# Attention and two MoE layers: the remainder `gl` of the activations subtracted on DVE in place of POOL

## The chip, the cores and the metric

The kernel runs on one core of a Trainium2 chip. The metric is the device time of one execution in microseconds (us), lower is better. Engines are named as in the profile: PE (TensorE matmul), PEld (its weight loads), DVE (VectorE), ACT (ScalarE), POOL (GpSimd), SP (SyncE, which issues most DMAs).

## The reference

Three layers follow each other: attention with a soft cap on its scores, a first MoE layer, and a second one with a softmax and a layer norm. The change lies in the first MoE layer, `_moe_ref`.

```python
def _moe_ref(x, w_in, w_out):          # x 1792x768, w_in 768x2048, w_out 2048x768
    h = x @ w_in
    g = h - np.tanh(h)
    return (g @ w_out).astype(np.float32)
...
    attn_out = _attn_ref(**attn_kwargs)                  # batch 4, 12 heads, 448 x 64
    x = attn_out.transpose(0, 2, 1, 3).reshape(B * S, H * D)
    x = _moe_ref(x=x, **moe_kwargs)
    return _moe2_ref(x=x, **moe2_kwargs)
```

All results are float32. The kernel gets float32-like precision from three matmuls in a shorter format (float32r): every operand `x` is split into a rounded part `xh` and the remainder `xl = x - xh`, and `x·w` is computed as `xh·wh + xl·wh + xh·wl`.

## The kernel before, in words

The 1792 tokens are worked in two halves of 896 (`hb` 0 and 1). Each half passes through `attention`, `moe1` and `moe2`, with x held transposed in SBUF (six pairs of tiles `xh`, `xl`, 128 x 896).

`moe1` cuts the 2048 hidden columns into four chunks `c` of 512. `up(c, half)` makes two hidden tiles each, so there are four tiles `hp` per chunk, each 128 hidden columns x 896 tokens, with 36 matmuls of 448 columns (lines 403 and 405). Chunk 0 is made by `first()` while the attention's last heads still finish. An `hp` lies in PSUM. Chunks 1 to 3 use the pool with the tag "a", which has two buffers, so the third tile of a chunk needs the buffer of the first, and PE waits until ACT and DVE have read that first tile for the last time.

`nonlinear(c, hp)` turns each `hp` into g. There are 4 chunks x 4 tiles x 2 halves = 32 calls. ACT makes `u` (line 431, square), `t` (433, tanh), the mask `mk` (435) and `w` (439). DVE makes `gf` in three steps: line 437 and line 440 read `hp` out of PSUM (440 is the last reader and sets the buffer free), line 441 reads `w` and `gf`, and line 442 copies `t` over `gf` where the mask says so. Then ACT rounds `gf` to `gh` (line 445), and the remainder `gl = gf - gh` is made at line 446. `gh` and `gl` have six buffers each, `gf`, `u`, `t` and `mk` two, `w` one.

`down(c)` multiplies the four pairs `gh`, `gl` of a chunk with `w_out` (lines 459 and 461, 24 matmuls for each of six row tiles `d`), and adds the result to `acc` (line 466 for chunk 0, line 468 on DVE for the others). The program order is `first`, then for each chunk `up(c+1)` before `down(c)`.

The weights come as float64 words. In the first half each unit of 128 x 512 is converted on the way: SP loads the words `st` (three buffers), DVE narrows them to `f` (lines 106, 107, 108), ACT rounds (line 114), DVE subtracts the rest (line 115), and SP stores the pair to DRAM (line 131, `keep`). There are 13 + 1 buffers `w` and `wx` for pairs. In the second half the stored pairs are only loaded (line 186). So DVE carries the conversions beside `nonlinear` in the first half and not in the second.

In `attention` the order of the instructions is written out by hand. In `moe1` and `moe2` a scheduler orders the instructions of each engine from the program order and its own estimates of durations; each engine then runs its own list strictly in order.

Of the kernel before, what the change touches and what calls it, by code (L numbers as in the profile page):

```python
# [9 lines left out]
F32 = mybir.dt.float32  # L10
# [4 lines left out]
ALU = mybir.AluOpType  # L15
# [14 lines left out]
def fused_kernel(ctx, tc, qk_in, v, cap, w1, w2, w3, w4, gln, out):  # L30
    nc = tc.nc
# [35 lines left out]
    def pst(name, tag="b"):  # L67
        return psum[tag].tile([P, 2, 512], F32, tag=tag, name=name)
# [128 lines left out]
    def load_w1(c, half):  # L197
        ts = []
        for i in range(NK // 2):
            ts += cols(unit(f"1_{c}_{half}_{i}", w1u[(c * 2 + half) * (NK // 2) + i], 2), 2)  # L200
        return ts

    def load_w2(c, d):
        return cols(unit(f"2_{c}_{d}", w2u[c * NK + d], CH // P), CH // P)
# [186 lines left out]
    def moe1(mp, xh, xl, yh, yl):  # L391
        acc = [mp.tile([P, HT], F32, tag=f"acc{d}", name=f"acc{d}", bufs=1) for d in range(NK)]
        gs = {}
        place.update(pool=(mp, WX1), at=-1)

        def up_mms(hp, wt, m, k0, k1, gg=(0, 1)):
            ms = slice(m * P, (m + 1) * P)
            for kk in range(k0, k1):
                wh, wl = wt[kk]
                xs = [(xh[kk][:, g * S:(g + 1) * S], xl[kk][:, g * S:(g + 1) * S]) for g in range(2)]  # L400
                for i in range(2):
                    for g in gg:
                        nc.tensor.matmul(hp[:, g, :S], wh[:, ms], xs[g][i], start=(kk == 0 and i == 0), stop=False)  # L403
                for g in gg:
                    nc.tensor.matmul(hp[:, g, :S], wl[:, ms], xs[g][0], start=False, stop=(kk == NK - 1))  # L405

        def first():

            gs[0] = []
            wts = [load_w1(0, 0), load_w1(0, 1)]  # L410
            hps = [pst("hp", "ab"[half]) for half in range(2) for _ in range(2)]
            for g, k0, k1 in ((0, 0, NK), (1, 0, 3), (1, 3, 4), (1, 4, 5), (1, 5, 6)):
                for m in range(3):
                    up_mms(hps[m], wts[m // 2], m % 2, k0, k1, (g,))
                    if k1 == NK and g == 1:
                        nonlinear(0, hps[m])
            up_mms(hps[3], wts[1], 1, 0, NK)
            nonlinear(0, hps[3])

        def up(c, half):  # L420
            gs.setdefault(c, [])
            wt = load_w1(c, half)
            for m in range(2):
                hp = pst("hp", "a")
                up_mms(hp, wt, m, 0, NK)
                nonlinear(c, hp)

        def nonlinear(c, hp):
            h = hp[:, :, :S]
            u = mp.tile([P, 2, S], F32, tag="u", name="u")  # L430
            nc.scalar.activation(u, h, AF.Square)
            t = mp.tile([P, 2, S], F32, tag="t", name="t")
            nc.scalar.activation(t, h, AF.Tanh)  # L433
            mk = mp.tile([P, 2, S], U8, tag="mk", name="mk")
            nc.scalar.activation(mk, t, AF.Square, scale=TS)
            gf = mp.tile([P, 2, S], F32, tag="gf", name="gf")
            nc.vector.scalar_tensor_tensor(gf, u, C2, h, ALU.mult, ALU.mult)  # L437
            w = mp.tile([P, 2, S], F32, tag="w", name="w", bufs=1)
            nc.scalar.activation(w, u, AF.Square, bias=gat)
            nc.vector.tensor_tensor(t, h, t, ALU.subtract)  # L440
            nc.vector.scalar_tensor_tensor(gf, w, GB, gf, ALU.add, ALU.mult)
            nc.vector.copy_predicated(gf, mk, t)
            gh = mp.tile([P, 2, S], F32R, tag="gh", name="gh", bufs=6)
            gl = mp.tile([P, 2, S], F32R, tag="gl", name="gl", bufs=6)
            nc.scalar.copy(gh, gf)  # L445
            nc.gpsimd.tensor_tensor(gl, gf, gh.bitcast(F32), ALU.subtract)  # L446
            gs[c].append((gh, gl))

        def down(c):
            for d in range(NK):  # L450
                wt = load_w2(c, d)
                op = pst("op")
                nm = CH // P
                for m in range(nm):
                    gg = gs[c][m]
                    wh, wl = wt[m]
                    for i in range(2):
                        for g in range(2):
                            nc.tensor.matmul(op[:, g, :S], wh, gg[i][:, g], start=(m == 0 and i == 0), stop=False)  # L459
                    for g in range(2):  # L460
                        nc.tensor.matmul(op[:, g, :S], wl, gg[0][:, g], start=False, stop=(m == nm - 1))  # L461
                for g in range(2):
                    cs = slice(g * S, (g + 1) * S)
                    a = acc[d][:, cs]
                    if c == 0:
                        nc.scalar.copy(a, op[:, g, :S])
                    else:
                        nc.vector.tensor_tensor(a, op[:, g, :S], a, ALU.add)  # L468
                    if c == NCHUNK - 1:
                        nc.scalar.copy(yh[d][:, cs], a)  # L470
                        nc.vector.tensor_tensor(yl[d][:, cs], a, yh[d][:, cs].bitcast(F32), ALU.subtract)

        first()
        for c in range(NCHUNK):
            if c + 1 < NCHUNK:
                up(c + 1, 0)
                up(c + 1, 1)
            down(c)
# [192 lines left out]
```

## Time and profile before

| what | value |
|---|---|
| time, median of 3 runs | 979.12 us (975.68 to 985.18) |
| profiled execution, its own time | 978.58 us |
| its span, first to last instruction | 976.6 us |
| granted TensorE clock, mean over the span | 0.99 of full speed |
| busy in the span: PE / DVE / ACT / POOL | 938.9 / 607.8 / 420.5 / 125.9 us |
| POOL's 32 subtractions at line 446 | 76.4 us, mean 2395 ns |

The span is that of the profiled execution; 2.0 us of its time lie around it. Busy time of an engine is the time in which at least one of its instructions ran. A granted clock of 1.00 is 2.4 GHz, and 0.50 would be 1.2 GHz; a mean between the two means that part of the stretch ran at the lower level.

### The profile page before, as it was taken

Reading aid. Unit: us, or ns where it says so; the run is one execution under the profiler, and the core shown is the slowest. Engines: PE = TensorE matmul, PEld = TensorE weight load, DVE = VectorE, ACT = ScalarE, POOL = GpSimd, SP = SyncE. Lnnn points to the kernel's source line nnn. Section 1 sums busy time; section 2 is a strip of 40 time slices with the busy share of each in tenths; the row PEclk is TensorE's granted clock in tenths of the full one; section 3 lists DMA queues with packets and bytes.
Section 4 is the critical chain, followed back from the end, with each engine's and each line's share of the span. In section 5 each row is a group of like instructions: output and inputs, shape, how many; then the busy total and the mean of one; then the engine's idle time right before and its main releaser. Section 6 shows DMA issues by size and latency. Waiting matters only on the chain.

```text
span 976.6 us, 11710 instructions
## 1 busy us (share of the span) xinstructions
PE 938.9 (96%) x4512; PEld 756.1 (77%) x4512; DVE 607.8 (62%) x914; ACT 420.5 (43%) x502; POOL 125.9 (13%) x123
## 2 busy tenths in 40 slices
PE   6999969899899999999989999999999999999998
PEld 3444449798899998888865555789999999988887
DVE  4687676998999997389415675596044352405751
ACT  6878506644624323243238775085251331212321
POOL 2221001302212120001011210032110201000000
PEclk9999989999999999999999999999999999999999
DMA  6564275279676575244135652242323332303311
GB/s 240 179 174 153 88 273 207 70 234 312 240 249 251 210 282 195 98 159 154 49 112 182 190 168 77 93 134 104 108 87 130 108 109 87 108 21 109 125 50 48
DMA packets 48947, 145.66 MB, mean 149 GB/s; under 512 B 11708, under 2 KB 16188, under 8 KB 48892
## 3 DMA queue, kind: packets, MB, share of 16 engines
q1 hardware_dynamic: 41404, 114.57, 34.0%
q0 software_dynamic: 7344, 30.35, 9.7%
q8 instruction: 35, 0.57, 0.2%
q14 instruction: 20, 0.16, 0.1%
q10 hardware_dynamic: 144, 0.00, 0.0%
HBM read 98.73 MB, written 43.33 MB: 145 GB/s over the span
## 4 chain that ended last, share of the span: by engine, by line
PE 82%; DMA 9%; DVE 5%; ACT 2%; issue 1%; SPq 0%; DVEq 0%; ACTq 0%
PE op L459 14%; PE hp L403 13%; PE o L308 8%; PE op L461 7%; PE hp L405 7%; DMA rs<-ou 4%; PE hp L222 4%; PE hp L221 4%; PE hp L220 4%; PE s L274 4%; PE oab L556 2%; PE oab L560 2%; PE oab L557 2%; DMA rd<-rs 2%; PE s L276 1%
## 5 line engine op out<-in xcount | busy, mean ns | idle before, releaser
L403 PE MATMUL hp<-xh,w 128*128 128x448 f32 x384 | 118.5, 377 | 18.2 <-DVE t L440 8.3
L446 POOL TENSOR_TENSOR gl<-gf,gh 128x896 fp32r<-128x896 f32 x32 | 76.4, 2395 | 418.6 <-ACT gh L445 389.9
L308 PE MATMUL o<-t,vf 128*65 128x448 f32 x288 | 116.8, 543 | 2.8 <-issue 1.4
L403 PE MATMUL hp<-xl,w 128*128 128x448 f32 x384 | 119.0, 376 | 0.4 <-DVE xl L357 0.4
L405 PE MATMUL hp<-xh,w 128*128 128x448 f32 x384 | 117.5, 373 | 0.0
L278 ACT ACTIVATE t<-s,tscale 128x896 f32<-128x896 f32 x96 | 82.4, 913 | 41.6 <-PE s L274 27.0
L459 PE MATMUL op<-gh,w 128*128 128x448 f32 x336 | 95.5, 366 | 0.0
L461 PE MATMUL op<-gh,w 128*128 128x448 f32 x336 | 95.4, 365 | 0.0
L459 PE MATMUL op<-gl,w 128*128 128x448 f32 x336 | 95.4, 365 | 0.0
L403 PEld LDWEIGHTS hp<-xh,w 128*128 128x128 f32 x384 | 73.7, 193 | 27.2 <-issue 10.8
L437 DVE SCALAR_TENSOR_TENSOR gf<-u,hp 128x896 f32<-128x896 f32 x32 | 34.8, 1087 | 80.2 <-ACT t L433 80.2
L308 PEld LDWEIGHTS o<-t,vf 128*65 128x65 f32 x288 | 37.6, 137 | 58.8 <-issue 47.8
L403 PEld LDWEIGHTS hp<-xl,w 128*128 128x128 f32 x384 | 74.3, 193 | 9.8 <-issue 1.7
L405 PEld LDWEIGHTS hp<-xh,w 128*128 128x128 f32 x384 | 73.9, 193 | 7.9 <-issue 1.5
L288 ACT ACTIVATE t<-t,shift,capt 128x1792 f32<-128x1792 f32 (+1 forms) x48 | 78.5, 1687 | 0.0
L468 DVE TENSOR_TENSOR acc<-op,acc 128x448 f32<-128x448 f32 x72 | 42.0, 621 | 52.2 <-PE op L461 52.2
L114 ACT CAST w<-f 128x512 fp32r<-128x512 f32 x44 | 27.1, 620 | 104.5 <-DVE f L108 50.7
L459 PEld LDWEIGHTS op<-gh,w 128*128 128x128 f32 x336 | 63.0, 188 | 5.3 <-DVE acc L468 0.4
L459 PEld LDWEIGHTS op<-gl,w 128*128 128x128 f32 x336 | 63.1, 188 | 5.0
L461 PEld LDWEIGHTS op<-gh,w 128*128 128x128 f32 x336 | 63.1, 188 | 5.0
L220 PE MATMUL hp<-w,xh 128*128 128x512 f32 x168 | 65.5, 390 | 0.0
L221 PE MATMUL hp<-w,xh 128*128 128x512 f32 x168 | 65.4, 389 | 0.0
(135 smaller groups left out, 1730.0 us busy)
## 6 DMA issues: line engine op xcount, KB each, us to landing
d<-w SPq DMA_DIRECT2D x69, 512.0 KB, 4.3
w<-d SPq DMA_DIRECT2D x56, 512.0 KB, 3.3
st<-in_moe_w_out_dram SPq DMA_DIRECT2D x35, 512.0 KB, 5.7
st<-in_moe_w_in_dram SPq DMA_DIRECT2D x24, 512.0 KB, 4.5
kq<-in_qk_dram POOLq DMA_DIRECT2D x21, 480.0 KB, 4.3
w<-d POOLq DMA_DIRECT2D x13, 512.0 KB, 5.4
vf<-in_v_dram POOLq DMA_DIRECT2D x24, 260.0 KB, 5.2
st<-in_moe_w_in_dram POOLq DMA_DIRECT2D x12, 512.0 KB, 6.4
```

The source lines that it names most:

```text
L220: nc.tensor.matmul(ps, sh, mh, start=first, stop=False)
L221: nc.tensor.matmul(ps, sh, ml, start=False, stop=False)
L222: nc.tensor.matmul(ps, sl_, mh, start=False, stop=last)
L278: nc.scalar.activation(t[:, 2 * r:2 * r + m], s[:, :m, :S], AF.Tanh, scale=tscale)
L288: nc.scalar.activation(t[:, sl], t[:, sl], AF.Exp, bias=shift, scale=capt)
L308: nc.tensor.matmul(o, vf[:, r + 5 * hh], t[:, 2 * r + hh], start=(r == 0), stop=False)
L403: nc.tensor.matmul(hp[:, g, :S], wh[:, ms], xs[g][i], start=(kk == 0 and i == 0), stop=False)
L405: nc.tensor.matmul(hp[:, g, :S], wl[:, ms], xs[g][0], start=False, stop=(kk == NK - 1))
L446: nc.gpsimd.tensor_tensor(gl, gf, gh.bitcast(F32), ALU.subtract)
L459: nc.tensor.matmul(op[:, g, :S], wh, gg[i][:, g], start=(m == 0 and i == 0), stop=False)
L461: nc.tensor.matmul(op[:, g, :S], wl, gg[0][:, g], start=False, stop=(m == nm - 1))
L468: nc.vector.tensor_tensor(a, op[:, g, :S], a, ALU.add)
```

## The change

One line changes: the subtraction that makes `gl` is issued to DVE in place of POOL. Its operands and result stay.

```diff
             gh = mp.tile([P, 2, S], F32R, tag="gh", name="gh", bufs=6)
             gl = mp.tile([P, 2, S], F32R, tag="gl", name="gl", bufs=6)
             nc.scalar.copy(gh, gf)
-            nc.gpsimd.tensor_tensor(gl, gf, gh.bitcast(F32), ALU.subtract)
+            nc.vector.tensor_tensor(gl, gf, gh.bitcast(F32), ALU.subtract)
             gs[c].append((gh, gl))
```

The scheduler lays the other instructions out anew around it. On DVE, in the first half, from the second tile of chunk 0 on, the order before is this (`hp_1071`, `hp_1072`, `hp_1073` are the second to fourth tile of chunk 0; `f` and `w` with numbers from 1637 up are weight conversions):

```order
L440 TENSOR_TENSOR t_1198<-hp_1071,t_1198 128x896
L441 SCALAR_TENSOR_TENSOR gf_1202<-w_1204,gf_1202 128x896
L106 TENSOR_SCALAR f_1676<-st_1674 128x512
L442 COPY_PREDICATED gf_1202<-mk_1200,t_1198 128x896
L437 SCALAR_TENSOR_TENSOR gf_1222<-u_1216,hp_1072 128x896
L440 TENSOR_TENSOR t_1218<-hp_1072,t_1218 128x896
L107 SCALAR_TENSOR_TENSOR f_1676<-st_1674,f_1676 128x512
L441 SCALAR_TENSOR_TENSOR gf_1222<-w_1224,gf_1222 128x896
L437 SCALAR_TENSOR_TENSOR gf_1275<-u_1269,hp_1073 128x896
L442 COPY_PREDICATED gf_1222<-mk_1220,t_1218 128x896
L440 TENSOR_TENSOR t_1271<-hp_1073,t_1271 128x896
```

At the same place the order now is this:

```order
L440 TENSOR_TENSOR t_1198<-hp_1071,t_1198 128x896
L446 TENSOR_TENSOR gl_1190<-gf_1182,gh_1189 128x896
L441 SCALAR_TENSOR_TENSOR gf_1202<-w_1204,gf_1202 128x896
L437 SCALAR_TENSOR_TENSOR gf_1222<-u_1216,hp_1072 128x896
L442 COPY_PREDICATED gf_1202<-mk_1200,t_1198 128x896
L440 TENSOR_TENSOR t_1218<-hp_1072,t_1218 128x896
L446 TENSOR_TENSOR gl_1210<-gf_1202,gh_1209 128x896
L441 SCALAR_TENSOR_TENSOR gf_1222<-w_1224,gf_1222 128x896
L437 SCALAR_TENSOR_TENSOR gf_1275<-u_1269,hp_1073 128x896
L442 COPY_PREDICATED gf_1222<-mk_1220,t_1218 128x896
L440 TENSOR_TENSOR t_1271<-hp_1073,t_1271 128x896
```

Each tile's `gl` stands behind the next tile's line 440, in a group of five that repeats up to the second tile of chunk 1, and the conversion instructions that stood between (L106, L107, later L115 and L108) have moved behind these groups.

On PE, at the border between the second and the third tile of chunk 1 in the first half (`hp_1340` and `hp_1394`), the order before is this:

```order
L403 MATMUL hp_1340<-xh_105,w_730 128x448 x2
L403 MATMUL hp_1340<-xl_111,w_730 128x448 x2
L405 MATMUL hp_1340<-xh_105,w_730 128x448 x2
L403 MATMUL hp_1394<-xh_100,w_799 128x448 x2
L403 MATMUL hp_1394<-xl_106,w_799 128x448 x2
```

Now it is this:

```order
L403 MATMUL hp_1340<-xh_105,w_730 128x448 x2
L403 MATMUL hp_1340<-xl_111,w_730 128x448 x2
L405 MATMUL hp_1340<-xh_105,w_730 128x448 x2
L459 MATMUL op_1502<-gh_1189,w_960 128x448 x2
L459 MATMUL op_1502<-gl_1190,w_960 128x448 x2
L461 MATMUL op_1502<-gh_1189,w_960 128x448
L403 MATMUL hp_1394<-xh_100,w_799 128x448 x2
L403 MATMUL hp_1394<-xl_106,w_799 128x448 x2
```

Five of the six matmuls with which `down(0)` begins have moved ahead of the third tile; the same holds in the second half. The rest of PE's order is unchanged.

## Rows read from the trace of the kernel before

**Rows 1.** The page, part 1: engines' busy us, share of span, instructions.
```profile
PE 938.9 (96%) x4512; PEld 756.1 (77%) x4512; DVE 607.8 (62%) x914; ACT 420.5 (43%) x502; POOL 125.9 (13%) x123
```

**Rows 2.** Timeline of PE, rows with waits in moe1: start, duration, [idle before <-releaser].
```profile
181.81 0.64 PE L403 MATMUL hp<-xh,w 128*128 128x448 f32 x2 [3.32 <-DVE t L440]
191.47 0.64 PE L403 MATMUL hp<-xh,w 128*128 128x448 f32 x2 [0.50 <-DVE t L440]
247.24 0.64 PE L403 MATMUL hp<-xh,w 128*128 128x448 f32 x2 [4.46 <-DVE t L440]
...
659.67 0.65 PE L403 MATMUL hp<-xh,w 128*128 128x448 f32 x2 [1.92 <-issue]
```

**Rows 3.** Timeline of DVE around the wait in the second half.
```profile
658.47 1.09 DVE L440 TENSOR_TENSOR t<-hp,t 128x896 f32<-128x896 f32 x1
```

**Rows 4.** Stretches behind PE's waits: length, busy by engine, PEclk, DMA share, GB/s.
```profile
181.80:187.10 5.30, 5.29 (x19) 4.79 (x20) 5.30 (x6) 3.12 (x4) 1.60 (x2) 0.68 0.30 89
...
247.20:254.70 7.50, 7.46 (x29) 6.84 (x30) 7.50 (x11) 5.37 (x7) 3.92 (x1) 0.77 0.72 223
...
659.70:667.10 7.40, 7.40 (x29) 6.76 (x30) 5.38 (x5) 3.53 (x4) 3.17 (x2) 0.77 0.08 30
```

**Rows 5.** The two stretches up to the long wait; busy PE, PEld, DVE, ACT, POOL.
```profile
156.70:199.00 42.30, 38.48 (x179) 34.47 (x178) 42.13 (x40) 30.28 (x36) 14.87 (x6) 0.96 0.24 86
199.00:247.20 48.20, 43.78 (x217) 40.23 (x215) 42.56 (x64) 21.94 (x35) 4.88 (x2) 1.00 0.87 289
```

**Rows 6.** Timeline of POOL, first subtraction of the first half.
```profile
162.76 2.13 POOL L446 TENSOR_TENSOR gl<-gf,gh 128x896 fp32r<-128x896 f32 x1 [67.82 <-ACT gh L445]
```

**Rows 7.** Timeline of DVE beside it.
```profile
160.04 1.22 DVE L442 COPY_PREDICATED gf<-mk,t 128x896 f32<-128x896 uint8 x1
161.14 1.08 DVE L437 SCALAR_TENSOR_TENSOR gf<-u,hp 128x896 f32<-128x896 f32 x1
162.13 1.09 DVE L440 TENSOR_TENSOR t<-hp,t 128x896 f32<-128x896 f32 x1
163.14 2.69 DVE L441 SCALAR_TENSOR_TENSOR gf<-w,gf 128x896 f32<-128x896 f32 x1
```

**Rows 8.** DVE by lines, 156.5 to 250 us: xcount, busy us, mean ns, idle before.
```profile
L108 DVE SCALAR_TENSOR_TENSOR f<-st,f 128x512 uint32<-128x512 uint32 x17 | 14.6, 859 | 0.2
L441 DVE SCALAR_TENSOR_TENSOR gf<-w,gf 128x896 f32<-128x896 f32 x9 | 14.4, 1604 | 0.1
L115 DVE TENSOR_TENSOR w<-f,w 128x512 fp32r<-128x512 f32 x16 | 14.1, 881 | 2.1 <-ACT w L114 2.1
L107 DVE SCALAR_TENSOR_TENSOR f<-st,f 128x512 uint32<-128x512 uint32 x18 | 13.5, 755 | 0.3
```

**Rows 9.** Single lines over the whole span: ns min/median/max of one instruction.
```profile
L441 DVE SCALAR_TENSOR_TENSOR gf<-w,gf x32: 1074/1092/3022, 157.9 to 795.8; 128x896 f32<-128x896 f32 x32
L440 DVE TENSOR_TENSOR t<-hp,t x32: 1072/1082/1120, 158.9 to 796.9; 128x896 f32<-128x896 f32 x32
L107 DVE SCALAR_TENSOR_TENSOR f<-st,f x72: 677/693/2608, 11.0 to 440.2; 128x512 uint32<-128x512 uint32 x72
L115 DVE TENSOR_TENSOR w<-f,w x44: 671/684/2629, 142.1 to 376.8; 128x512 fp32r<-128x512 f32 x44
L445 ACT CAST gh<-gf x32: 938/944/953, 161.7 to 819.6; 128x896 fp32r<-128x896 f32 x32
```

**Rows 10.** Timeline of DVE ahead of the long wait.
```profile
243.07 0.42 DVE L106 TENSOR_SCALAR f<-st 128x512 uint32<-128x512 uint32 x1
243.41 1.08 DVE L437 SCALAR_TENSOR_TENSOR gf<-u,hp 128x896 f32<-128x896 f32 x1
244.41 0.68 DVE L107 SCALAR_TENSOR_TENSOR f<-st,f 128x512 uint32<-128x512 uint32 x1
245.01 1.08 DVE L441 SCALAR_TENSOR_TENSOR gf<-w,gf 128x896 f32<-128x896 f32 x1
246.01 1.08 DVE L440 TENSOR_TENSOR t<-hp,t 128x896 f32<-128x896 f32 x1
```

**Rows 11.** Weight words `st`, 140 to 260 us: issue to landing.
```profile
DMA to landing us min/median/max: 4.2/5.7/10.9
```

## The prediction

> **What bounds the kernel now.** I read the page's busy times first: PE is busy for 938.9 of 976.6 us, DVE for 62%, POOL for 13% [rows 1]. So PE sets the end, and a change on DVE or POOL counts only where PE waits for it. Next I went through PE's timeline for its waits in the first MoE layer. There are four [rows 2]: 3.32, 0.50 and 4.46 us in the first half, all released by line 440 on DVE, the last reader of an `hp` tile, and 1.92 us in the second half. The page labels the last one "issue", but line 440 ran until 658.47 + 1.09 = 659.56 [rows 3], just before PE went on at 659.67, so I count it with the others. Together they make 10.20 us. The third view is the granted clock behind these waits [rows 4]: after the three longer ones PE ran for a while at the lower of its two levels (1.2 in place of 2.4 GHz), with means of 0.68, 0.77 and 0.77. That costs 5.30 x 0.32 + 7.50 x 0.23 + 7.40 x 0.23 = 1.7 + 1.7 + 1.7 = 5.1 us more. After the wait of 0.50 us I count none. All that can be won here is thus 15.3 us.
>
> Why is DVE late? In the stretch up to the first two waits it is busy for 42.13 of 42.30 us [rows 5]. But its instructions are not all of their usual length. When POOL makes the first `gl` (162.76 to 164.89 [rows 6]), line 441, which starts at 163.14, takes 2.69 us [rows 7], against a median of 1.09 over the kernel [rows 9]. Line 440, one of whose inputs lies in PSUM, never takes more than 1.12 us [rows 9]. So POOL's subtraction holds up those DVE instructions that read two operands from SBUF.
>
> **What the change removes.** Up to 250 us there are eight `gl` on POOL. The slowed lines, mean against median [rows 8, 9]: L441 9 x (1.604 - 1.092) = 4.6; L115 16 x (0.881 - 0.684) = 3.2; L108, with L107's median as it has the same shape, 17 x (0.859 - 0.693) = 2.8; L107 18 x (0.755 - 0.693) = 1.1. That is 11.7 us, 1.5 us for each `gl`.
>
> **What it adds.** The trace has no DVE `gl`. The nearest row is L441, of the same shape with two inputs from SBUF: 1.07 us at its fastest, 1.09 in the median, 1.60 as the mean of the stretch with slowed ones [rows 8, 9]. Nothing on POOL is left in this layer to slow it, so I take the median. Consecutive instructions overlap a little: from L437 to L440 to L441 the starts lie 0.99 and 1.01 us apart [rows 7], so a `gl` occupies DVE for 1.0 us (bounds 1.0 to 1.5). Each also waits for `gh`. The cast on ACT takes 0.94 us [rows 9], and POOL took up the result at 162.76, about 0.1 us behind its end (161.7 + 0.94 [rows 6, 9]). In the new order, line 440 of the next tile stands between line 442 and the `gl`, which covers 1.0 of that. I count 0 to 0.1 us a `gl`, if ACT is free.
>
> By the Trainium skill (Perfetto Trace Analysis, Optimizing Scalar/DVE Operations), work may be moved off a saturated DVE, even to GPSIMD, and that advice speaks against this change. The same passage adds that the two share a port, and SBUF — State Buffer (Who interferes with whom) says that a DVE instruction with two SBUF inputs and a GpSimd one that reads SBUF exclude each other for a whole instruction. By that L441 at 163.14 would end about 1.09 us behind 164.89, so after 2.84 us; 2.69 were measured [rows 7], and the trace agrees with the second rule.
>
> **Place 1, third tile of chunk 1, first half (181.81).** The DVE order in the change section runs without conversions from line 440 at 162.13. Up to line 440 of chunk 1's first tile come 15 instructions, which start 0.99 to 1.10 us apart (1.10 behind L442 [rows 7]): 163.1 + 11 x 1.0 + 3 x 1.1 = 177.4 for the start, 178.5 for the end, 178.8 with three waits for `gh`. PE finishes the second tile at 181.81 - 3.32 = 178.5, and now has five matmuls of `down(0)` to do first, about 1.0 us (36 matmuls of one tile take some 7.4 us [rows 4]). It asks for the buffer at 179.5, 0.7 us after it is free. The wait goes, and with it the slow clock, and the 0.50 behind it. Gain 3.3 + 1.7 + 0.5 = 5.5 us. The five matmuls themselves are only moved.
>
> **Place 2, third tile of chunk 2 (247.24).** PE now arrives 5.5 us earlier, at 242.8 - 5.5 = 237.3. DVE has, up to line 440 (start 246.01 [rows 10]): 11.7 us of slowing less, 8 `gl` = 8.0 us more, and fewer conversion instructions ahead of it. Counted in the two orders, 34 L106, 34 L107, 33 L108, 19 L115 stood before it, and 31, 31, 31, 17 do now. With 0.34 for an L106 and 0.60 for the others (starts at 243.07, 243.41; 244.41, 245.01 [rows 10]) this is 3 x 0.34 + 7 x 0.60 = 5.2 us. Line 440 ends 8.9 us earlier, at 238.2, and PE waits 0.9 in place of 4.46 us. This supposes that the weight words come in time: the DMA engines are 0.87 busy here [rows 5], and a load takes 5.7 us in the median and 10.9 at most [rows 11]. I take a wait of 1.5 to 2 us and half of the slow clock: 4.46 + 1.7 - 1.8 - 0.8 = 3.6 us gained.
>
> **Later in the first half.** DVE stays nearly full up to the end of chunk 3, and PE comes 9 us earlier than before. The conversions that were put behind must be done here, but POOL's last six subtractions stop slowing DVE too. I take 0.5 us of new waits (0 to 3).
>
> **Place 3, second half (659.67).** The order is the same without conversions, so place 1's reckoning holds: 1.9 + 1.7 = 3.6 us gained.
>
> Sum: 5.5 + 3.6 - 0.5 + 3.6 = 12.2 us. 978.58 - 12.2 = 966.4, made against the profiled execution, which is 0.54 us under the median of the runs shown, so I round to 966.5. POOL's 76 us are worth nothing by themselves: nobody waits for POOL.
>
> **Rivals.**
>
> *The loads set the pace.* Three buffers of `st` make a conversion wait for a landing, and with landings towards 10.9 us [rows 11] in place of 5.7 the 11 loads between place 1 and place 2 (four rounds of three) take 4 x 2.3 = 9 us more than DVE needs, which eats the 8.9 us. Then PE reaches 247.24 as before, the first half gains nothing, and only 3.6 us of the second remain: 975. For it: the DMA share of 0.87 and DVE's 5.6 us of idle time in that stretch [rows 5]. Against: DVE then slept for little of it, and the worst landing is one of many.
>
> *DVE blocks itself (slower).* An in-order DVE that reaches a `gl` before its `gh` stands still, with line 440 of later tiles and the conversions queued behind, and PE waits for these. This happens where ACT has other work between line 442 and the cast, one or two instructions of about 0.9 us. The 12 `gl` up to chunk 3's first tile, each delayed by 2 us, cost 24 us, against about 8 us that DVE saves there (as at place 2: 8.9 us after eight `gl`): 16 us more in the first half, less 3.6 in the second: 991. It decides from about 0.7 us a `gl` on (8/12); the new order, with a line between 442 and the `gl`, speaks against.
>
> *The load alone counts.* If the long L441 had another cause than POOL, DVE would get 8 us of `gl` and no relief up to place 2, less the 5.2 us of conversions put behind: it would be 2.8 us later there, and 3 us (three `gl`) later at places 1 and 3. With 2 x 3 + 3 that makes 988. Rows 7 and 9 speak against it.
>
> *Nothing measurable.* The two long waits reappear elsewhere in the first half, as DVE is full there either way, and new small waits eat the second half's gain: 979.
>
> **How the numbers follow.** A measurement of this kernel tells about 1% from no change. 1% under the median is 969.3. Forecast (963 if every wait goes, 978.58 - 15.3, to 972): 0.56, of which 0.46 lies under 969.3. The loads: 0.18, within 1%. Nothing measurable: 0.12, within 1%. DVE blocks itself: 0.10, slower. The load alone: 0.04, of which 0.02 is slower by over 1% (988 lies at 0.9%). So faster 0.46; slower 0.12; within 1% 0.42. The range reaches from 962 to 978: it takes in the forecast and the loads' case and leaves out the last three, of which the nothing case lies at its edge. The forecast's own range is 963 to 972.
>
> **What would show it.** Right: L441, L107, L108 and L115 at 1.09, 0.69 and 0.68 us without outliers; L446 on DVE at about 1.09; no wait of PE for L440 near 179 and near 657; a short one near 238; clock 1.00 behind them. Wrong: L446 rows on DVE with idle time released by line 445; new PE waits between 250 and 320; a wait near 238 to 247 of several us with DVE idle for `st`.

## The result and the profile after

| | before | after |
|---|---|---|
| time, median | 978.83 us (973.42 to 985.18, 6 runs) | 965.97 us (961.69 to 968.56, 6 runs) |
| ratio, 95% interval | | 0.9894 (0.9862 to 0.9926) |
| profiled execution, its time / span | 978.58 / 976.6 us | 963.42 / 961.1 us |
| granted TensorE clock, mean of the span | 0.990 | 0.996 |

The changed kernel is faster by 1.1%. The forecast was 966.5 us in a range of 962 to 978.

The page's first part, which answers to [rows 1]: POOL's 75.8 us are gone, and DVE has only 4.2 us more, although it does 32 more instructions of 1.09 us (34.9 us). The missing 30.7 us are time that DVE's older instructions no longer take.

```profile
PE 935.8 (97%) x4512; PEld 751.5 (78%) x4512; DVE 612.0 (64%) x946; ACT 420.6 (44%) x502; POOL 50.1 (5%) x91
```

That is seen line by line in the single lines of DVE over the whole span (ns min/median/max of one instruction), which answer to [rows 9]. The medians are the same as before to about 1%, but the maxima of 2.6 to 3.0 us are gone. The new line 446 takes what line 441 takes.

```profile
L441 DVE SCALAR_TENSOR_TENSOR gf<-w,gf x32: 1070/1086/1114, 150.4 to 780.4; 128x896 f32<-128x896 f32 x32
L107 DVE SCALAR_TENSOR_TENSOR f<-st,f x72: 667/685/719, 11.0 to 428.3; 128x512 uint32<-128x512 uint32 x72
L115 DVE TENSOR_TENSOR w<-f,w x44: 669/684/711, 134.9 to 366.5; 128x512 fp32r<-128x512 f32 x44
L446 DVE TENSOR_TENSOR gl<-gf,gh x32: 1070/1092/1101, 155.7 to 805.1; 128x896 fp32r<-128x896 f32 x32
```

PE's timeline has three waits for line 440 in the first half's MoE layer, 2.86 us in all, and none in the second half. Before there were four with 10.20 us [rows 2].

```profile
230.79 0.65 PE L403 MATMUL hp<-xh,w 128*128 128x448 f32 x2 [0.27 <-DVE t L440]
292.87 0.64 PE L403 MATMUL hp<-xh,w 128*128 128x448 f32 x2 [2.32 <-DVE t L440]
300.67 0.64 PE L403 MATMUL hp<-xh,w 128*128 128x448 f32 x2 [0.27 <-DVE t L440]
```

The two stretches of [rows 5] in windows of the same length (columns: length, busy PE, PEld, DVE, ACT, POOL, then PEclk, DMA share, GB/s): PE is busy for all of the first one, at full clock. DVE is as full as before.

```profile
156.70:199.00 42.30, 42.30 (x207) 38.41 (x206) 41.55 (x50) 28.48 (x37) 0.00 (x0) 1.00 0.21 73
199.00:247.20 48.20, 47.93 (x233) 43.24 (x232) 43.67 (x67) 26.11 (x39) 0.00 (x0) 1.00 0.84 286
```

**Two profiles are not the whole comparison.** The spans differ by 15.5 us, the medians by 12.9. PE's longest wait for `xh`, at the end of the first attention, was 7.30 us in the profile of before and 3.62 in that of after, in code whose order is the same in both, before any `gl` is made. PE's timeline, first kernel before, then the kernel after:

```profile
143.14 1.12 PE L403 MATMUL hp<-xh,w 128*128 128x448 f32 x2 [7.30 <-DVE xh L356]
```

```profile
136.00 1.11 PE L403 MATMUL hp<-xh,w 128*128 128x448 f32 x2 [3.62 <-DVE xh L356]
```

So I compare stretches that begin behind this wait. "First half" below is the time from that matmul to the first matmul of line 220, where the second MoE layer begins (380.40 before, 367.90 after); "second half" is the same in the other half. By this the change gained 5.4 us in the first half (237.3 to 231.9) and 4.3 in the second (226.2 to 221.9) in the first pair of profiles, and the other 5.8 us lie elsewhere.

### The profile page after: what moved, and what is told of

Read it like the earlier page. It is cut to its first block, busy times and chain, and to the rows that moved or that the text cites. A ratio compares the mean times of both kernels' runs of the same rounds, so it can differ in the third digit from the quotient of the medians.

```text
span 961.1 us, 11645 instructions
## 1 busy us (share of the span) xinstructions
PE 935.8 (97%) x4512; PEld 751.5 (78%) x4512; DVE 612.0 (64%) x946; ACT 420.6 (44%) x502; POOL 50.1 (5%) x91
## 4 chain that ended last, share of the span: by engine, by line
PE 73%; DVE 15%; DMA 8%; ACT 2%; issue 2%; SPq 0%; DVEq 0%; ACTq 0%
PE hp L403 11%; PE o L308 10%; PE op L459 8%; PE hp L405 5%; PE s L274 5%; PE op L461 4%; PE hp L222 4%; PE hp L221 4%; PE hp L220 4%; PE oab L556 3%; PE oab L560 3%; PE oab L557 3%; DMA st<-in_moe_w_out_dram 2%; DVE f L107 2%; DVE f L108 2%; DMA st<-in_moe_w_in_dram 2%
## 5 line engine op out<-in xcount | busy, mean ns | idle before, releaser
L403 PE MATMUL hp<-xh,w 128*128 128x448 f32 x384 | 116.7, 372 | 7.7 <-DVE xh L356 4.8
L405 PE MATMUL hp<-xh,w 128*128 128x448 f32 x384 | 115.8, 368 | 0.0
L403 PEld LDWEIGHTS hp<-xh,w 128*128 128x128 f32 x384 | 72.3, 190 | 16.5 <-DVE xh L356 6.0
L405 PEld LDWEIGHTS hp<-xh,w 128*128 128x128 f32 x384 | 72.6, 189 | 7.7 <-issue 1.5
L222 PE MATMUL hp<-w,xl 128*128 128x512 f32 x168 | 65.5, 390 | 0.3 <-DVE xl L471 0.3
L431 ACT ACTIVATE u<-hp 128x896 f32<-128x896 f32 x32 | 29.5, 921 | 79.4 <-PE hp L405 79.3
```

The lines of the kernel that those rows point to most:

```text
L222: nc.tensor.matmul(ps, sl_, mh, start=False, stop=last)
```

## The experiments

There were twelve runs, in four groups, each group beside runs of the kernel before on the same chip. The two stretches are those of the profiled execution.

| run | `gl` on | ratio to before (95%) | first half | second half | PE's waits for line 440, first / second half |
|---|---|---|---|---|---|
| before | POOL | 1 | 237.3 | 226.2 | 8.3 / 1.9 |
| e7 before again | POOL | single execution | 235.6 | 225.9 | 7.3 / 2.3 |
| after | DVE | 0.9894 (0.9862 to 0.9926) | 231.9 | 221.9 | 2.9 / 0 |
| e1 after again | DVE | 0.9892 (0.9853 to 0.9931) | 228.4 | 221.9 | 0 / 0 |
| e8 after, third trace | DVE | single execution | 228.1 | 223.5 | 2.3 / 0 |
| e2 | DVE, then POOL | 0.9954 (0.9922 to 0.9985) | 229.7 | 229.3 | 0.8 / 3.4 |
| e3 | POOL, then DVE | 0.9979 (0.9957 to 1.0001) | 237.4 | 225.6 | 7.1 / 0 |
| e4 | DVE, and POOL too | 1.0221 (1.0185 to 1.0257) | 250.3 | 228.9 | 12.7 / 4.6 |
| e5 | nobody | 0.9807 (0.9759 to 0.9855) | 223.6 | 223.5 | 0 / 0 |
| e6 | DVE twice | 0.9835 (0.9791 to 0.9878) | 224.9 | 222.1 | 0 / 0 |
| e9 | POOL, `down` first | 0.9957 (0.9934 to 0.9980) | 236.9 | 223.3 | 6.2 / 0 |
| e10 | DVE, `down` first | 0.9827 (0.9801 to 0.9854) | 223.9 | 226.2 | 0.3 / 0 |
| e12 e10 again | DVE, `down` first | 0.9811 (0.9767 to 0.9855) | 223.7 | 227.7 | 0 / 0 |
| e11 | DVE, `down` first in all | 0.9840 (0.9805 to 0.9876) | 228.0 | 221.9 | 0 / 0 |

(The wait that the timeline labels "issue" at chunk 1's third tile in the second half is counted with line 440, as in the prediction.)

### Again, unedited: e1, e7, e8

> The changed kernel once more, unedited, beside new runs of the kernel before. In the first pair of profiles the two traces differ by 7.5 us before any gl is made: the first line 437 of the first half starts at 156.73 us before and at 149.24 us after, with the order of the attention unchanged. Theory A (that part is no effect of the change but how two single executions differ): the first line 437 of this profile lies anywhere between 149 and 157 us, and the median gain stays at 10 to 15 us, of which the MoE layers' own waits and slow clock give 8 to 12. Theory B (the change also shortens the attention, in a way I don't see): the first line 437 is again within 1 us of 149.24. Either way lines 441, 107, 108 and 115 stay under 1.15, 0.73, 0.73 and 0.72 us at their longest.

> The kernel before, for a second trace of it. If the late part of the first attention differs from execution to execution, PE's longest wait for xh is either near 3.2 to 3.8 us or near 7.3 us, as in the six profiles so far, and the first half's MoE layer takes 236 to 239 us either way, with waits for line 440 of 3 to 5 us at the same two matmuls as in the first trace. If those waits were an accident of the first trace, they are gone.

> The changed kernel, for a third trace. The first half's MoE layer takes 228 to 232 us, the second half's 221 to 226 us, whatever PE's longest wait for xh (3.2 to 3.8 or about 7.3 us). Matmuls of one pair of 448 columns start either 202.7 or 206.7 ns apart at a granted clock of 1.00, as in the profiles so far, and change from the one to the other only at a wait of PE or where PE goes over from one line to another.

The second trace of before has the waits at the same three matmuls (PE's timeline), with a granted clock of 0.77 and 0.64 in the 7.4 us behind the first two (windows, columns as above):

```profile
174.67 0.63 PE L403 MATMUL hp<-xh,w 128*128 128x448 f32 x2 [3.95 <-DVE t L440]
238.22 1.08 PE L403 MATMUL hp<-xh,w 128*128 128x448 f32 x2 [3.39 <-DVE t L440]
...
653.30 1.08 PE L403 MATMUL hp<-xh,w 128*128 128x448 f32 x2 [2.30 <-issue]
```

```profile
174.60:182.00 7.40, 7.33 (x29) 6.70 (x30) 7.40 (x8) 3.35 (x4) 2.24 (x1) 0.77 0.22 71
238.20:245.60 7.40, 7.38 (x24) 6.66 (x25) 7.40 (x11) 5.36 (x7) 3.93 (x1) 0.64 0.76 232
```

So they belong to the kernel. The first half took 235.6 us, 0.4 us under the range that I had expected. The wait for `xh` does not belong to the kernel: it was 4.15 us here, which is neither of the two values that I had expected. Over all fourteen traces it was 7.3 us twice (before and e2, 978.58 and 980.2 us) and 3.1 to 5.0 us in the others, on either side of the change. e1 alone does not decide between its theories, as its first line 437, at 150.1 us, fits both. The other traces do: it started at 149.4 us with the kernel before (e7) and at 155.9 us with `gl` on DVE (e2), so theory A holds. In e1 lines 107 and 108 reached 0.753 us at most and line 115 0.739, a little over what I expected, but no instruction was held up.

With e2 and e3 (below) there are three traces with `gl` on POOL and four with it on DVE for each half, in the scheduler's own order. In the mean the first half takes 236.7 us with POOL (before, e7, e3) and 229.5 with DVE (after, e1, e8, e2): 7.2 us gained. The second half takes 227.1 (before, e7, e2) and 223.2 (after, e1, e8, e3): 3.9 us gained.

### One half at a time: e2, e3

```diff
-            nc.vector.tensor_tensor(gl, gf, gh.bitcast(F32), ALU.subtract)
+            (nc.vector if hb == 0 else nc.gpsimd).tensor_tensor(gl, gf, gh.bitcast(F32), ALU.subtract)
```

e3 has the two engines exchanged.

> gl by DVE in the first half of the columns only, by POOL in the second. By the prediction's steps the first half brings 5.5 + 3.6 - 0.5 = 8.6 of 12.2 us, so about 970 us (with the first pair of traces, where the first half's MoE layer gained 5.0 us only, 974), and PE's wait for line 440 in the second half is still there (about 1.9 us, with a stretch at a lower granted clock behind it). Rival, the loads set the first half's pace: 979, and all the gain is in the second half.

> gl by POOL in the first half, by DVE in the second only. By the prediction's steps 3.6 us of gain, so about 975 us: PE's waits of 3.3 and 4.5 us for line 440 stay in the first half, the one of 1.9 us in the second goes. If the gain comes from anything but these waits and the clock behind them, no such split: under 971 or over 979.

Measured: 970.35 and 973.39 us beside 976.12, ratios 0.9954 and 0.9979. The waits split as the theory says. With POOL in the second half only (e2), PE waits there:

```profile
657.26 0.64 PE L403 MATMUL hp<-xh,w 128*128 128x448 f32 x2 [2.35 <-issue]
665.85 0.65 PE L403 MATMUL hp<-xh,w 128*128 128x448 f32 x2 [1.06 <-DVE t L440]
```

With POOL in the first half only (e3), the two long waits of before stand there, and none in the second half:

```profile
174.26 0.90 PE L403 MATMUL hp<-xh,w 128*128 128x448 f32 x2 [3.51 <-DVE t L440]
238.04 0.64 PE L403 MATMUL hp<-xh,w 128*128 128x448 f32 x2 [3.62 <-DVE t L440]
```

The rival of the loads (no gain in the first half) falls with e2's first half of 229.7 us. In times the parts come to 4.5 and 2.0 us, together 6.5 where both at once gave 10.5 (0.9892). The intervals, 2 to 4 us wide on either side for each of the three, leave room for that; the section on the hardware shows another share of it, in e3's second half. e2's 4.5 us (1.5 to 7.6 by its interval) lie under the 8.6 us that were forecast for the first half; by the stretches the first half gained 7.2.

### The hold alone and the load alone: e4, e5, e6

e4 lets DVE make `gl`, and POOL subtract the same two tiles once more, into `u`, which nobody reads after that.

```diff
             nc.vector.tensor_tensor(gl, gf, gh.bitcast(F32), ALU.subtract)
+            nc.gpsimd.tensor_tensor(u, gf, gh.bitcast(F32), ALU.subtract)
```

> gl by DVE, and POOL makes the same subtraction of the same two tiles once more, into a tile that nobody reads afterwards: DVE keeps the new load and POOL's hold on it comes back. PE's order differs from that of the changed kernel by one matmul at the place of the first wait. Theory (POOL's subtraction lengthens DVE instructions with two SBUF operands, 1.5 us for each gl, on top of 1.0 us of load): lines 441, 107, 108, 115 have maxima of 2 to 3 us again, the new line 446 on DVE too, and the time is 985 to 990 us, over the kernel before. Rival (the long instructions had another cause than POOL, and the load is cheap): no outliers, 966 us.

Measured: 996.07 us, 2.2% over before and more than expected. Lines 107 and 108 reached only 1.6 us, lines 441, 115 and 446 2.6 to 3.0. PE does ten matmuls of `down(0)` ahead of chunk 1's third tile in the first half, five more than in the changed kernel and not one, and waited for line 440 all the same. POOL's hold is back, and now it also falls on the new instruction, as both wait for the same `gh`. POOL's timeline, then DVE's, of e4:

```profile
156.82 2.13 POOL L446 TENSOR_TENSOR u<-gf,gh 128x896 f32<-128x896 f32 x1 [61.83 <-ACT gh L445]
...
157.19 2.70 DVE L446 TENSOR_TENSOR gl<-gf,gh 128x896 fp32r<-128x896 f32 x1
159.81 1.08 DVE L441 SCALAR_TENSOR_TENSOR gf<-w,gf 128x896 f32<-128x896 f32 x1
```

The DVE instruction ends at 159.89, 0.94 us after POOL's end at 158.95. The Trainium skill (SBUF — State Buffer, Summary: rules for kernel authors) says that where a DVE instruction has two SBUF inputs and the GpSimd one reads SBUF, the second to issue is fully blocked until the first finishes; by that the end would lie at about 158.95 + 1.09 = 160.04, and the trace agrees within 0.15 us. Over the kernel, line 446 on DVE took 1.92 us in the mean (61.5 us for 32) in place of 1.09, POOL's subtraction 2.70.

The hold is not all that e4 adds. `u` has two buffers, and POOL now uses them last, so ACT's square at line 431 waited for POOL nine times, 21.4 us in all (the waits of ACT: total, times, longest):

```profile
ACT u L431 <- POOL u L446: 21.4, 9, 3.1
```

How the 20 us divide between the hold and these waits is not shown.

e5 makes no `gl` at all, and multiplies by `gh` twice.

```diff
-            nc.vector.tensor_tensor(gl, gf, gh.bitcast(F32), ALU.subtract)
-            gs[c].append((gh, gl))
+            gs[c].append((gh, gh))
```

> No engine makes gl: the remainder is left out of the computation, and down() multiplies by gh a second time in its place, so that TensorE has the same number of matmuls. Relief from POOL's hold without DVE's load. Measured from PE's first matmul behind its longest wait for xh to line 220's first matmul, the first half's MoE layer took 237.3 and 237.4 us with gl on POOL and 228.4, 229.7 and 231.9 us with gl on DVE. Theory (after the change DVE is no longer what PE waits for, but for 0 to 3 us): 222 to 231 us, and a time 0 to 4 us under that of the changed kernel, near 960 to 966. Rival (DVE's load of 1.0 us a gl still sets the first half's pace): 8 to 12 us under the changed kernel, near 955.

Its order on PE is that of the kernel before, and on DVE nearly so, so it shows what POOL's hold alone had cost: all waits for line 440 are gone, and the time is 959.46 us. Against the changed kernel the first half is 6 us shorter (223.6 against 229.5), between the theory and the rival. The times do not decide: 2.9 us under e1's median, and about 8 us by the two ratios, whose intervals touch.

e6 makes `gl` twice on DVE, one instruction behind the other.

```diff
             nc.vector.tensor_tensor(gl, gf, gh.bitcast(F32), ALU.subtract)
+            nc.vector.tensor_tensor(gl, gf, gh.bitcast(F32), ALU.subtract)
```

> DVE makes each gl twice over into the same tile, POOL none: twice the load (2.0 us of DVE a gl), no hold by POOL. By the prediction's steps three more gl up to the places 1 and 3 bring DVE 3 us later there, where it had 0.7 us to spare: waits of about 2.3 us, and 1.7 us of slow clock behind each; eight more up to place 2 and a PE 4 us later there give a wait of 5 us with 1.7 behind it. That is 4.0 + 6.7 + 4.0 = 15 us over the changed kernel, 974 to 982 us, about the kernel before. Rival (it is not the microseconds of DVE that count but that the work was on POOL at all): within 3 us of the changed kernel. Lines 441, 107, 108 and 115 have no outliers in either.

Here my theory failed, and the rival came nearer: 959.99 us, *under* the changed kernel, by 2.4 us against e1's median and by 5.6 by the ratios. The intervals overlap, so whether the rival's 3 us were missed is open. The windows of e6 show DVE fuller than ever and PE without a pause up to 250 us:

```profile
150.00:250.00 100.00, 100.00 (x495) 92.68 (x494) 98.16 (x123) 62.98 (x83) 0.00 (x0) 1.00 0.44 153
250.00:360.00 110.00, 109.38 (x540) 101.11 (x540) 106.99 (x174) 39.29 (x56) 1.60 (x3) 1.00 0.72 249
```

I had left the order as it was and only added the time. But the scheduler lays PE's and DVE's lists out anew when DVE has more to do. Matmuls of `up` (U) and `down` (D) in PE's list in the first half, from chunk 0 on, and the instructions of lines 106, 107, 108, 115 that stand on DVE ahead of line 440 of chunk 2's first tile (place 2):

```
                    PE's list                         106 107 108 115   gl ahead
before              U288 D144 U144 D144 U144 D288      34  34  33  19    0 (POOL)
e5, nobody          U288 D144 U144 D144 U144 D288      34  34  33  19    0
after               U216 D5  U72 D139 U144 D144 ...    31  31  31  17    8
e6, DVE twice       U216 D20 U72 D124 U144 D144 ...    28  28  28  14   16
```

Each round of eight `gl` puts ten to twelve conversion instructions behind, and in e6 PE does 20 matmuls of `down(0)` (4.1 us) before it asks for the buffer of chunk 1's third tile, where the changed kernel does 5. POOL's hold appears in no such plan: the counts of before and of e5 are the same.

### The order alone: e9 to e12

If so, the order should be worth something by itself. The kernels e9 (`gl` on POOL) and e10 (on DVE) write the first sixth of `down(0)`, 24 matmuls, ahead of the last two tiles of `up(1)`; the loads stay in their order. e11 does the same at each chunk.

```diff
-        def up(c, half):
+        def up(c, half, wt):
...
-            wt = load_w1(c, half)
...
-        def down(c):
-            for d in range(NK):
+        def down(c, ds):
+            for d in ds:
...
-                up(c + 1, 0)
-                up(c + 1, 1)
-            down(c)
+                up(c + 1, 0, load_w1(c + 1, 0)); wt = load_w1(c + 1, 1)
+                down(c, range(1 if c == 0 else 0)); up(c + 1, 1, wt)
+            down(c, range(1 if c == 0 else 0, NK))
```

> gl on POOL as before; only the order is changed: the first of six parts of down(0), 24 matmuls, is written ahead of the last two tiles of up(1), so that PE does it before it asks for the buffer of chunk 1's third tile. The kernel that makes gl twice on DVE had 20 of these ahead in the first half (25 in the second) and no wait for line 440. Theory A (where PE asks for the buffer decides, and POOL's hold and DVE's load only set when it is free): 24 matmuls are 4.9 us, so the waits of 3.3 to 4.0 us in the first half and 1.9 to 2.4 us in the second at this place go, with 1.7 us of slow clock each; the wait at chunk 2's third tile stays or grows, as PE comes 5 us earlier there. Gain 3.6 + 3.6 less up to 2, so 969 to 973 us against 976 to 979. Theory B (order is without influence, DVE's own microseconds count): 974 to 979.

> gl on DVE once, with the order of the run before this one: 24 matmuls of down(0) ahead of chunk 1's third tile. Theory A (the doubled gl was as fast as it was because the order that it brought leaves DVE more time before PE asks): no waits for line 440 but small ones at chunk 3, the first half's MoE layer 223 to 228 us, and a time like that of the doubled gl, 957 to 962. Theory B (the three traces of the changed kernel have so few waits at chunk 1 and 2 that the order gives nothing more): 962 to 966, like the changed kernel.

> As the run before this one, with 24 matmuls of down(c) ahead of the third tile of chunk c + 1 at all of the chunks. It takes away what was left of waits for line 440 at chunks 2 and 3 (0 to 2.6 us in the three traces of the changed kernel). Theory A: 0 to 2 us under the run before this one, 955 to 962. Rival (the weights of down(c) are now wanted before they are converted, so PE waits for line 115 in place of line 440): slower than the run before this one.

> The kernel with gl on DVE and 24 matmuls of down(0) ahead once more, for a second set of times and a second trace. If it is better than the changed kernel by where PE asks for the buffers, the ratio to the kernel before is again 0.980 to 0.986 (the changed kernel: 0.989), no wait for line 440 over 1 us stands in the first half's MoE layer, and each half's MoE layer takes 222 to 224 us where matmuls start 202.7 ns apart and 226 to 228 us where they start 206.7 ns apart. If the first set of four times was luck: 0.987 to 0.991.

e9 came out at 971.49 us, as theory A said: the waits at places 1 and 3 are gone, but PE comes to place 2 earlier, and DVE, with POOL's hold and all its conversions in front, does not. PE's timeline of e9, and the window behind the wait:

```profile
239.30 1.08 PE L403 MATMUL hp<-xh,w 128*128 128x448 f32 x2 [6.23 <-DVE t L440]
```

```profile
239.30:246.70 7.40, 7.40 (x26) 6.69 (x27) 7.37 (x10) 4.84 (x6) 3.59 (x1) 0.67 0.76 281
```

In the first half PE also waited 0.34 us for a `gl` of POOL and twice, 1.6 us in all, for line 466 on ACT. That half is 236.9 us, no better than before; the gain is in the second half (227.1 to 223.3), which has no place 2 of this kind. e10 came out at 960.22 us, and again (e12) at 959.19: one wait of 0.32 us in the first half's MoE layer in the one trace and none in the other. By the times this version beats both kernels, by 1.7 to 1.9% against before. The changed kernel's ratio of 0.9892 lies outside the intervals of e10 and e12, and theirs outside its own. The traces do not show where these 6 to 8 us come from. Both MoE layers together took 450.1 and 451.4 us in e10 and e12, and 453.8, 450.3 and 451.6 us in the three of the changed kernel, whose waits for line 440 were 2.9, 0 and 2.3 us. So theory A has the waits right, but that they make the whole gain is not shown. e11 (0.9840) tells no difference from e10, and neither theory's bound is decided: where e10 has 0.3 us of waits there is nothing left to take away.

With the orders of e10 and e6 the load on DVE costs less than these runs can tell apart: no `gl` (e5) 0.9807, one 0.9827 and 0.9811, two 0.9835, with intervals that overlap. e9 and e10 have the same list of `up` and `down` on PE and differ in the engine of `gl`, with DVE's list laid out around it: POOL 0.9957, DVE 0.9827.

## Why the prediction was right, point by point

**What bounds: right.** All that can be won was put at 15.3 us. e5, which takes away the hold and adds nothing, gained 16.8 us between the medians (976.30 to 959.46), or 14 to 24 by its interval, which takes in 15.3.

**Removed, 11.7 us of slowing: right, but the rule was too narrow.** Without POOL's subtraction (after, e1, e5, e6, e8) no line has an outlier; with it they return (e2, e3, e4, e9). The prediction says that instructions with two operands from SBUF are held up. In the trace of before line 106, which reads only `st` from SBUF, was held up too, once: it took 2.24 us in place of its median of 0.42. DVE's timeline, then POOL's:

```profile
349.36 2.24 DVE L106 TENSOR_SCALAR f<-st 128x512 uint32<-128x512 uint32 x1
...
348.79 2.53 POOL L446 TENSOR_TENSOR gl<-gf,gh 128x896 fp32r<-128x896 f32 x1 [28.64 <-DVE acc L468]
```

Line 442 was held up once as well (3.00 us at 654.60). Both lie behind 250 us, so the 11.7 us stand.

**Added, 1.0 us a `gl` and 0 to 0.1 us for `gh`: right.** One took 1.09 us. The chain of waits behind DVE gives 25.3 us of waiting for `gh` over the kernel, seven times, 19.2 of them in one piece; but up to 250 us, where DVE is full, the ten `gl` had 0.2 us of idle time before them (columns: xcount, busy us, mean ns, idle before).

```profile
DVE gl L446 <- ACT gh L445: 25.3, 7, 19.2
```

```profile
L446 DVE TENSOR_TENSOR gl<-gf,gh 128x896 fp32r<-128x896 f32 x10 | 10.9, 1090 | 0.2
```

So the rival in which DVE blocks itself is refuted.

**Place 1: right to a few tenths.** The trace of after is 7.5 us earlier throughout (first line 437 at 149.24 against 156.73). With that, line 440 of chunk 1's first tile was forecast to start at 169.9, and PE to ask at 172.0, 0.7 us after its end. DVE's timeline, then PE's:

```profile
170.20 1.09 DVE L440 TENSOR_TENSOR t<-hp,t 128x896 f32<-128x896 f32 x1
...
171.67 0.37 PE L461 MATMUL op<-gh,w 128*128 128x448 f32 x1
171.88 0.57 PE L403 MATMUL hp<-xh,w 128*128 128x448 f32 x2
```

The margin was 171.88 - 171.29 = 0.59 us. It is thin: it is less than three `down` matmuls, and five had been moved ahead. Behind the waits in these traces PE goes on 0.10 to 0.15 us after line 440's end. It did so 0.15 us behind it in e8 and e2 too, and 0.14 us behind it at place 3 of after, so in those cases next to no margin was left. (The time of the five matmuls, 1.0 us, is right, but [rows 4] shows 29 matmuls in 7.40 us at a clock of 0.77, not 36.)

**Place 2: the mechanism right, the wait oversized.** By the same shift line 440 was to end at 230.7, with a wait of 0.9 us. It ended at 230.64, and PE, which asked at 230.52 and not at 229.8, waited 0.27:

```profile
229.56 1.08 DVE L440 TENSOR_TENSOR t<-hp,t 128x896 f32<-128x896 f32 x1
```

I had taken 1.5 to 2 us and half of the slow clock instead, for the weight loads. The traces show 0.27, 0, 0.82 and 0 us (after, e1, e8, e2), and a granted clock of 1.00 in the stretch from 199.00 to 247.20. The allowance was not needed here, and the rival of the loads falls at this place. (Its 2.3 us for each round of three loads are worked out from no row.)

**Later in the first half: undersized.** 0.5 us of new waits were taken. At chunk 3 it was 2.59, 0, 1.49 and 0.81 us (after, e1, e8, e2), 1.2 in the mean. Here the loads do count: ahead of PE's wait at 292.87 in after, DVE stood 3.37 us for weight words, more than PE then waited. ACT's tiles for chunk 3's first tile were ready at 285.80, and behind this stop DVE worked without a break up to the end of its line 440 at 292.72. In e1, e8 and e2 DVE stood 1.6, 1.4 and 2.5 us at this place. DVE's timeline of after:

```profile
287.50 0.43 DVE L106 TENSOR_SCALAR f<-st 128x512 uint32<-128x512 uint32 x1 [3.37 <-DMA st<-in_moe_w_out_dram]
```

**Place 3: right.** The wait is gone in all traces with DVE in the second half.

**The sum.** 8.6 us were forecast for the first half and 3.6 for the second. The stretches give 7.2 and 3.9: 11.1 in place of 12.2, beside 10.4 and 10.5 us by the ratios of after and e1 and 12.9 between the first medians. So the mechanism and the size hold, but that 966.5 met 965.97 within 0.5 us is partly luck: the first medians lie further apart than the ratios.

**What I did not see.** Two things that the experiments brought out. First, I treated the 5 matmuls moved ahead and the conversions put behind as side effects, and took each DVE microsecond ahead of line 440 as one lost. e6 shows that the plan answers to more load on DVE, and the equal plans of before and e5 that it does not answer to POOL's hold; in e6 the second `gl` cost nothing that could be measured. Second, the rival "the load alone counts" (988 us) had the wrong mechanism: load without hold (e6) is no slower than the change, and load with hold (e4) is worse than its price, since the hold fell on the new instruction too and ACT waited for POOL.

## What to carry to other kernels

Look at the longest instruction of a line beside its median: where DVE instructions that read SBUF have outliers of twice their time, and POOL runs a subtraction across them, the work on POOL is not free, and 1.0 us of DVE can be cheaper than 2.1 us of POOL. The scheduler here planned around the load of an engine and not around one engine holding up another, so check its plan against the trace. Then look at where the waiting engine asks: with 24 matmuls put ahead of a buffer's request the times fell by another 0.7 to 0.8%, though the traces do not show where all of it comes from.

## What the runs showed of the hardware that I had not expected

**Two paces of PE at the same clock.** Pairs of matmuls of 448 columns start either 405 or 413 ns apart, 202.7 or 206.7 ns a matmul, both at a granted clock of 1.00, for tens of microseconds on end. e10 runs nearly all of its first half at the one pace and its second half at the other. PE's timeline of e10, six pairs in 2.43 us and six in 2.48 us:

```profile
259.71 0.57 PE L459 MATMUL op<-gh,wx 128*128 128x448 f32 x2
...
262.14 0.57 PE L459 MATMUL op<-gh,wx 128*128 128x448 f32 x2
...
699.64 0.57 PE L403 MATMUL hp<-xl,w 128*128 128x448 f32 x2
...
702.12 0.57 PE L403 MATMUL hp<-xl,w 128*128 128x448 f32 x2
```

The same stretch of the second half, PE busy without a break at a clock of 1.00, in e10 and then in e11: 1018 and 1038 matmuls.

```profile
620.00:830.00 210.00, 210.00 (x1018) 190.72 (x1017) 108.17 (x122) 78.35 (x98) 0.00 (x0) 1.00 0.31 106
```

```profile
620.00:830.00 210.00, 210.00 (x1038) 194.59 (x1037) 110.04 (x124) 80.05 (x100) 0.00 (x0) 1.00 0.33 110
```

A half at the slow pace takes 4 us more: second halves without waits are 221.9 to 223.5 us at 202.7 ns and 226.2 and 227.7 at 206.7. This is why e3's second half (225.6, at 206.7 from about 652 us on) has no wait and yet gains little, and why the first half of e1 and e11, without waits for line 440, takes 228 us where e5, e6, e10 and e12 take 224 to 225. Some 2 us of what these gain on the changed kernel's mean of 229.5 us is thus the pace (an estimate: about half of the 1092 matmuls of those four first halves ran 4 ns slower), and no effect of the kernel that is shown. Most changes of pace fall on a wait of PE: at 238.04 in e3 it went to the slow pace, at 292.87 in after to the fast one. In e10 one came near 236.6 us without a wait. Executions of one kernel differ (after and e1 begin the first half at 206.7 ns, e8 at 202.7). It gives back some of what a removed wait brings, or adds to it. What sets it I have not found.

**Executions of one kernel spread by 1%.** The twelve times of after and e1 lie between 960.3 and 969.4 us. The longer wait for `xh` (3.7 us more) and the slow pace (4 us a half) are of that size, but only the profiled executions show them; that they are the cause is not shown.
